# Chunked attention into a leaky-ReLU feed-forward: first-layer products of blocks 5 to 8, sums in PSUM, and a new step order

## The chip, the cores and the metric

The kernel runs on one core of a Trainium2 chip. The time of a run is the device time of that core in microseconds (us). A run can be taken with a hardware profile; the profile's span goes from the first to the last instruction of the program, so the time of a run is a little longer than a span.

Five engines matter here. TensorE (PE in the profile, PEld for its weight loads) multiplies and writes only to PSUM, a small memory of eight banks that each hold 512 float32 numbers in each of 128 partitions. VectorE (DVE), ScalarE (ACT) and GpSimd (POOL) do elementwise work on the main on-chip memory, SBUF; the first two also read and write PSUM. SyncE (SP) issues transfers. POOL also issues those transfers that convert float32 to float16.

## The reference

```python
# q, k, v: (8 batches, 8 heads, 576, 64); chunks of 64 rows attend to themselves
scores = scale * np.matmul(q_c, k_c.transpose(0, 1, 2, 4, 3))
scores = scores - np.max(scores, axis=-1, keepdims=True)
attn = np.exp(scores)
attn = attn / (np.sum(attn, axis=-1, keepdims=True) + 1e-09)
out = np.matmul(attn, v_c)
# then x = out as (4608 tokens, 512 features)
h = x @ w_in                      # 512 -> 2048
g = np.maximum(0.01 * h, h)
return (g @ w_out).astype(np.float32)   # 2048 -> 512
```

## The kernel before

The 4608 tokens are worked in two rhythms. Attention goes by groups u = 0 to 35 of 128 tokens (two chunks of all eight heads). The feed-forward part goes by blocks j: two of 128 tokens, then 17 of 256 (`BLOCKS`, line 46), so a block from 2 on takes two groups.

A group passes through these steps, each a function and a letter of the order: `g` loads q and k with a conversion to float16; `tq` and `tk` transpose them on TensorE, `q` and `k` copy the transposes out of PSUM (from group 14 on the DMA transposes instead, `tdq` and `tdk`, and `cq` copies q into a buffer padded with zeros); `s` is the score product; `m`, `b`, `x`, `z`, `n` are maximum, subtraction, exponential, sum with reciprocal, and normalisation; the softmax is transposed either on TensorE (`e`, with a copy `c`) or by the DMA (`d`); `v` is the product with v, and `a` copies it into `xT`, the ring of transposed tokens. The steps `e`, `c` are used for groups 0 to 5 and `d` from group 6 on. `y` and `w` write zeros into the padded buffers at the start, and `i` multiplies ones into an unused bank: i33 stands for 33 units of 128 columns, in matmuls of up to three units. All `i` steps stand ahead of the first step of the first layer.

The second layer of blocks 2 to 18 uses seven block products in place of eight (the Strassen form of Winograd): `sum` forms four sums of the hidden values (SG, line 203), `R` is one product of 8 matmuls over 256 columns (`product`, line 205), `comb` copies or adds the parts (`combine`, line 251). The first layer uses it from block 9 on (`W0`, line 50): `xs` forms four sums of tokens, `V` is one product for one half s of the hidden features (`wide`, line 389, 8 matmuls over 128 columns), 14 to a block. There, products 1, 6, 7 and 4 add up in one bank, and after each of the first three `lx` (line 442) copies the running sum to SBUF (`xkeep`); products 2, 5 and 3 go to other banks and `la` (line 449) adds the kept copies to them on VectorE; `lp` and the last `lx` apply the leaky ReLU. Blocks 0 to 8 compute the first layer plainly: `A` and `M` (`mm1`, line 311) and the leaky ReLU `H` and `G` (`act1`, line 328). For blocks 5 to 8 that is eight steps M of 8 matmuls over 256 columns.

Nothing schedules at run time. The string `ORDER` (line 735) lists the steps, the program issues them in that order, and each engine works through its own instructions in that order, waiting where an operand is not ready. The loads of the first nine groups and of the weights are issued from a list of their own ahead of it (`LOADS`, line 142). PSUM is cut up by hand: four banks for products are dealt out by the digits of `BANKS` (line 154), and the other four belong to q transposes, k transposes, scores, and the softmax with its product, which products share in some blocks.

Of the kernel before, what the change touches and what calls it, by code (L numbers as in the profile page):

```python
# [16 lines left out]
def kernel(  # L17
# [24 lines left out]
    VL = (4, 5, 6, 7)  # L42
    UX = 9
    G = 2 * CH

    BLOCKS = 2 * [128] + 17 * [256]
    EARLY = (2, 3, 4)
    LAST = len(BLOCKS) - 1
    HF, HM = NFC // 2, d_model // 2
    W0 = 9  # L50
    AMID = range(W0, 17)
    ONE = EARLY + tuple(range(16, len(BLOCKS)))
    ZMM = range(W0 - 2, 16)

# [3 lines left out]


# [5 lines left out]
    xT = sbp.tile([128, NT, RING], FP16, name="xT")  # L65
    qk: dict[int, tuple[bass.AP, bass.AP]] = {}

    made: set[tuple] = set()

    def need(*what):  # L70
        assert what in made, what

    def load_qk(u):

        both = []
        for name, src in (("q_in", q), ("k_in", k)):
# [18 lines left out]
    def load_v_heads(b, m, h0, h1):  # L95
        if b >= NVB:
            need("batch", b - NVB)
        nc.gpsimd.dma_start(  # L98
            out=VB[b % NVB][m * CH:(m + 1) * CH, h0:h1, :, m * CH:(m + 1) * CH].rearrange("p h c d -> p (h c) d"),
            in_=v[b, m * H // 2 + h0:m * H // 2 + h1].rearrange("h (c j) d -> j (h c) d", j=CH),  # L100
        )

    def load_v(b):
        for m in range(2):
            load_v_heads(b, m, 0, H // 2)

    def load_w_in(f0, f1):
        for m in range(2):
            nc.gpsimd.dma_start(
                out=w_inT[m * CH:(m + 1) * CH, :, f0:f1],  # L110
                in_=moe_w_in[m * d_model // 2:(m + 1) * d_model // 2, f0:f1].rearrange("(t d) f -> d t f", d=D),
            )

    def load_w_in_quarter(a):
        load_w_in(512 * a, 512 * a + 512)

    def load_w_out_quarter(a):
        load_w_out(4 * a, 4 * a + 4)
# [33 lines left out]


    BANKS = (
        "01230123012301230123023123103210310231023102320132132013213021302132103120312031023102310320323123131232121321"
        "31321323213212132131321323213210213021320130201321"
    )
    banks = iter(BANKS)

    def mm():  # L160
        return "m" + next(banks)

    TW: dict[int, bass.AP] = {}
    SG: dict[tuple[int, int], bass.AP] = {}
    bank: dict[tuple[int, str], bass.AP] = {}
    kept: dict[tuple[int, str], bass.AP] = {}
    opened: set[tuple[int, str]] = set()

    def weight_sum(n):
        b11, b12 = w_outT[:, :HF, :HM], w_outT[:, :HF, HM:]  # L170
        b21, b22 = w_outT[:, HF:, :HM], w_outT[:, HF:, HM:]
        x, y = {1: (b12, b11), 2: (b22, TW.get(1)), 3: (b22, b12), 4: (b21, TW.get(2))}[n]
        TW[n] = sbp.tile([128, HF, HM], FP16, name=f"TW{n}")
        nc.vector.tensor_tensor(out=TW[n], in0=x, in1=y, op=ALU.subtract)

    def rows(j):

        nh = BLOCKS[j] // 2
        halves_of = slice(0, nh), slice(nh, 2 * nh)
        return halves_of[::-1] if j in EARLY else halves_of  # L180

    def token_sums(j, n):
        if (j, n) in SG:
            return
        if j in EARLY:
            for a, p in {
                1: [(a, 1) for a in range(4)], 2: [(0, 2), (1, 2)], 3: [(0, 1), (1, 1), (0, 2), (1, 2)], 4: [(2, 2), (3, 2)],
            }[n]:
                need("act", j, a, p)
        if n in (2, 4):  # L190
            token_sums(j, n // 2)
        nh = BLOCKS[j] // 2
        one, two = rows(j)
        a11, a12 = gT[j][:, :HF, one], gT[j][:, HF:, one]
        a21, a22 = gT[j][:, :HF, two], gT[j][:, HF:, two]
        SG[j, n] = sbp.tile([128, HF, nh], FP16, name="SG", tag="gS", bufs=4, padded_shape=[128, HF, 128])
        x, y, op = {
            1: (a21, a22, ALU.add),
            2: (SG.get((j, 1)), a11, ALU.subtract),
            3: (a11, a21, ALU.subtract),  # L200
            4: (a12, SG.get((j, 2)), ALU.subtract),
        }[n]
        (nc.gpsimd if (j, n) in SG_POOL else nc.vector).tensor_tensor(out=SG[j, n], in0=x, in1=y, op=op)  # L203

    def product(j, n, i):
        one, two = rows(j)
        g, w = gT[j], w_outT
        where, left, right = {
            1: ("X", g[:, :HF, one], w[:, :HF, :HM]),
            2: ("W", g[:, HF:, one], w[:, HF:, :HM]),  # L210
            3: ("Z", SG.get((j, 4)), w[:, HF:, HM:]),
            4: ("X", g[:, HF:, two], TW.get(4)),
            5: ("Z", SG.get((j, 1)), TW.get(1)),
            6: ("X", SG.get((j, 2)), TW.get(2)),
            7: ("X", SG.get((j, 3)), TW.get(3)),
        }[n]
        if where != "X" and j in ONE:
            where = n
        if (j, where) not in bank:
            tag = None if j in EARLY else {"X": "qp", "Z": None if j in ZMM else "kp"}.get(where)  # L220
            bank[j, where] = psp.tile([128, 2, HM], FP32, name=f"pr{where}", tag=tag or mm(), bufs=1)
        to = bank[j, where]
        if j == LAST and n == 4:
            last_product(left, right)
            return
        for f in range(HF):
            nc.tensor.matmul(  # L227
                out=to[:, i, :],
                lhsT=left[:, f, i * 128:(i + 1) * 128],
                rhs=right[:, f, :],  # L230
                start=(j, where) not in opened,
# [119 lines left out]
    def w_in_sum(n):  # L351
        if len(WS) >= n:
            return
# [519 lines left out]
```

## Time and profile before

| What | Value |
|---|---|
| Median of three runs | 275.13 us (274.96 to 275.59) |
| Span of the profiled execution | 273.3 us |
| First layer begins | 17.44 us |
| Instructions | 9009 |
| HBM read, written | 36.70 MB, 9.44 MB |

The profile gives the span alone for its execution; the runs' times also hold what lies around it. An engine's busy time counts compute only. A matmul's end is modelled, and the next one starts before it, so the step from one start to the next, not a matmul's own length, is what a matmul costs.

### The profile page before, as it was taken

To read this page: it belongs to the slowest core of one execution; us is meant where nothing else is said; L and a number is where in the kernel's file an instruction comes from. 1 tells how busy PE (TensorE), PEld (TensorE's weight loads), DVE (VectorE), ACT (ScalarE), POOL (GpSimd) and SP (SyncE) were. 2 spreads that over 40 slices of the span, in tenths; PEclk is the share of its full clock that TensorE was granted. 3 is DMA by queue.
4 is the path that set the end of the run, shared out by engine and by line. 5 is a ranking of instruction groups with operands and counts; after the bars stand their busy time and mean duration, and the time that the engine had idled before them with its cause. 6 is when DMAs were issued, how large, how long until landed. Compare 5 with 4: busy or idle time off the path is not lost.

```text
span 273.3 us, 9009 instructions
## 1 busy us (share of the span) xinstructions
PE 265.9 (97%) x3705; PEld 242.4 (89%) x3705; DVE 219.9 (80%) x427; ACT 208.8 (76%) x410; POOL 165.3 (60%) x190
## 2 busy tenths in 40 slices
PE   7889999999999999999999999999999999999994
PEld 3579958999999899998989999999999998999994
DVE  7786869999997668798677987977899879488783
ACT  6667635665779688666999989899999998857560
POOL 8848546783175448649689799689895636012100
PEclk9999999999999999999999999999999999999999
DMA  9999999999999999999999999799999503131113
GB/s 147 155 188 191 206 178 156 176 117 130 210 138 169 171 140 119 195 219 168 164 189 153 203 160 124 139 134 180 95 147 158 134 2 101 22 98 40 41 41 115
DMA packets 159241, 38.34 MB, mean 140 GB/s; under 512 B 150240, under 2 KB 154720, under 8 KB 159200
## 3 DMA queue, kind: packets, MB, share of 16 engines
q0 software_dynamic: 111392, 18.10, 98.3%
q1 hardware_dynamic: 46768, 19.41, 38.7%
q8 instruction: 29, 0.48, 0.7%
q10 hardware_dynamic: 1040, 0.26, 0.4%
q14 instruction: 12, 0.10, 0.2%
HBM read 36.70 MB, written 9.44 MB: 169 GB/s over the span
## 4 chain that ended last, share of the span: by engine, by line
PE 86%; DVE 5%; ACT 3%; POOL 3%; issue 2%; POOLq 0%; DVEq 0%; ACTq 0%
PE hT L319 20%; PE prX L227 20%; PE xbank L416 11%; PE xpr L416 9%; PE prZ L227 6%; PE pr L227 6%; PE prW L227 3%; PE Sp L584 3%; PE xp L656 3%; PE oP L462 3%; ACT QZ L539 1%; ACT gT L435 1%; PE kp L512 1%; PE qp L512 1%; POOL SG L203 1%
## 5 line engine op out<-in xcount | busy, mean ns | idle before, releaser
L319 PE MATMUL hT<-xT,w_inT 128*128 128x128 f16 (+1 forms) x768 | 62.4, 237 | 0.0
L319 PEld LDWEIGHTS <-w_inT 128*128 128x128 f16 x768 | 53.6, 98 | 2.8
L227 PEld LDWEIGHTS <-SG 128*128 128x128 f16 x544 | 51.0, 98 | 5.4
L620 POOL TENSOR_TENSOR en<-ex,zi 128x512 f16<-128x512 f16 x26 | 28.2, 1085 | 40.1 <-DVE zi L614 19.8
L453 DVE TENSOR_TENSOR xkeep<-xpr,xkeep 128x512 f32<-128x512 f32 x60 | 39.6, 681 | 13.7 <-ACT xkeep L447 9.6
L333 ACT ACTIVATE gT<-hT 128x512 f16<-128x512 f32 x64 | 36.6, 595 | 9.0 <-PE hT L319 8.9
L227 PEld LDWEIGHTS <-gT 128*128 128x128 f16 x400 | 37.3, 98 | 4.3 <-ACT gT L435 0.4
L447 ACT ACTIVATE xkeep<-xbank 128x512 f32<-128x512 f32 x60 | 34.6, 593 | 7.4 <-PE xbank L416 7.0
L416 PEld LDWEIGHTS <-WS 128*128 128x128 f16 x640 | 38.0, 98 | 0.5
L91 POOL DMA_DIRECT2D q_in<-in_q_dram x39 | 33.4, 861 | 7.0 <-DMA w_outT<-in_moe_w_out_dram 3.0
L91 POOL DMA_DIRECT2D k_in<-in_k_dram x39 | 32.6, 838 | 7.8 <-DMA VB<-in_v_dram 3.3
L227 PE MATMUL prX<-TW,SG 128*128 128x256 f16 x272 | 35.3, 273 | 0.0
L435 ACT ACTIVATE gT<-xkeep 128x512 f16<-128x512 f32 x56 | 33.4, 631 | 2.1 <-DVE xkeep L453 1.8
L260 ACT ACTIVATE keep<-prX 128x256 f32<-128x256 f32 x51 | 19.6, 384 | 16.9 <-PE prX L227 16.5
L416 PEld LDWEIGHTS <-w_inT 128*128 128x128 f16 x480 | 29.0, 98 | 0.9 <-issue 0.4
L203 DVE TENSOR_TENSOR SG<-gT 128x1024 f16<-128x1024 f16 x34 | 25.2, 740 | 4.7 <-ACT gT L333 2.9
L610 DVE TENSOR_REDUCE z<-ex 128x8 f32<-128x512 f16 x36 | 24.4, 679 | 4.9 <-ACT ex L604 4.7
L593 DVE TENSOR_REDUCE mx<-Sp 128x8 f32<-128x512 f32 x36 | 24.4, 677 | 4.5 <-PE Sp L584 4.5
L573 ACT ACTIVATE QZ<-QT 64x512 f16<-64x512 f16 x44 | 27.3, 627 | 0.9 <-PE Sp L584 0.3
L677 ACT ACTIVATE xT<-xp 128x512 f16<-128x512 f32 x36 | 21.5, 596 | 6.0 <-PE xp L656 5.8
L387 POOL TENSOR_TENSOR xs<-xT 128x256 f16<-128x256 f16 x18 | 12.5, 701 | 20.7 <-ACT xT L677 20.7
L98 POOL DMA_DIRECT2D VB<-in_v_dram x24 | 23.4, 987 | 0.0
(92 smaller groups left out, 486.0 us busy)
## 6 DMA issues: line engine op xcount, KB each, us to landing
out_dram<-osb SPq DMA_DIRECT2D x35, 256.0 KB, 4.1
q_in<-in_q_dram POOLq DMA_DIRECT2D x31, 128.0 KB, 5.9
k_in<-in_k_dram POOLq DMA_DIRECT2D x31, 128.0 KB, 6.7
VB<-in_v_dram POOLq DMA_DIRECT2D x8, 288.0 KB, 9.1
VB<-in_v_dram POOLq DMA_DIRECT2D x16, 144.0 KB, 5.3
w_inT<-in_moe_w_in_dram POOLq DMA_DIRECT2D x8, 256.0 KB, 7.2
w_outT<-in_moe_w_out_dram POOLq DMA_DIRECT2D x4, 512.0 KB, 11.6
q_in<-in_q_dram POOLq DMA_DIRECT2D x8, 64.0 KB, 6.3
```

What stands on the lines that cost most here:

```text
L91: nc.gpsimd.dma_start(out=to, in_=rows)
L203: (nc.gpsimd if (j, n) in SG_POOL else nc.vector).tensor_tensor(out=SG[j, n], in0=x, in1=y, op=op)
L227: nc.tensor.matmul(out=to[:, i, :], lhsT=left[:, f, i * 128:(i + 1) * 128], rhs=right[:, f, :], start=(j, where) not in opened, stop=(f == ...
L319: nc.tensor.matmul(out=hT[:, i, :], lhsT=w_inT[:, t, fc * 128:(fc + 1) * 128], rhs=xT[:, t, r0:r0 + tb], start=(t == 0), stop=(t == NT - 1),)
L333: nc.scalar.activation(out=gT[j][:, nf * a:nf * a + nf, c0:c0 + tb], in_=HT.pop((j, a, p)), func=AFT.Prelu, bias=0.0, scale=1.0, alpha=0.01,)
L416: nc.tensor.matmul(out=to[:, i, :], lhsT=left[:, t, i * 128:(i + 1) * 128], rhs=right[:, t], start=(n in (1, 2, 5) and t == 0 and i == 0), ...
L435: nc.scalar.activation(out=gT[j][:, f0:f0 + 4, hi * 128:hi * 128 + 128], in_=of, func=AFT.Prelu, bias=0.0, scale=1.0, alpha=0.01)
L447: nc.scalar.activation(out=XK[j, s, n], in_=XB[j, s], func=AFT.Copy, bias=0.0, scale=1.0)
L453: nc.vector.tensor_tensor(out=to, in0=of, in1=to, op=ALU.add)
L573: nc.scalar.activation(out=to, in_=QT[u][part], func=AFT.Copy, bias=0.0, scale=1.0)
L593: nc.vector.tensor_reduce(out=MX[u], in_=SP[u], axis=AXL.X, op=ALU.max)
L620: (nc.gpsimd if u >= UP else nc.vector).tensor_tensor(out=E[u], in0=ex, in1=ZI.pop(u).unsqueeze(2).to_broadcast((128, 8, CH)), op=ALU.mult)
```

## The change

The program is rewritten so that every tile's place is read from one string. The eight PSUM banks form one pool, and the digits of `BANKS` name the bank of each PSUM tile and the slot of each rotating SBUF tile. A step that ends in `'` goes to its second engine: VectorE in place of ScalarE for copies and the leaky ReLU, POOL in place of VectorE for `n`, `xs` and `sum`, ScalarE in place of VectorE for the small add `z.1` and for the zeros `y`. `z` is split into three steps. Blocks 0 to 4 keep plain first layers, and blocks 5 to 18 use seven products. `e` and `c` serve groups 0 to 8, and `d` the others.

In the seven products, the first product is copied into a second PSUM bank (`ls`), onto which product 2 is then accumulated; product 5 is copied to SBUF (`lf`); `la` with 3 adds the running sum to it and writes that into the bank on which product 3 is then accumulated, and `la` with 7 adds the running sum once more in SBUF. The four results go through the leaky ReLU as they stand (`lp`).

```diff
-    W0 = 9
-    ONE = EARLY + tuple(range(16, len(BLOCKS)))
+    LATE = (2, 3, 4)
+    FIVE = (2, 3, 4, 16, 17, 18)
...
+    def copy(other, to, of):
+        if other:
+            nc.vector.tensor_copy(out=to, in_=of)
         else:
+            nc.scalar.activation(out=to, in_=of, func=AFT.Copy, bias=0.0, scale=1.0)
...
-        if n in (1, 6, 7, 4):
-            if n == 1:
-                tag = "kp" if s else "Sp"
-                if j in AMID:
-                    tag = "m0" if s else "kp"
-                XB[j, s] = psp.tile([128, 4, 128], FP32, name="xbank", tag=tag, bufs=1)
-            to = XB[j, s]
-        elif n == 3:
-            to = XM[j, s, n] = XM[j, s, 5]
-        else:
-            to = XM[j, s, n] = psp.tile([128, 4, 128], FP32, name="xpr", tag=mm(), bufs=1)
+        if n == 1:
+            XB[j, s] = ps([128, 4, 128], "xbank")
+        elif n == 5:
+            XZ[j, s] = ps([128, 4, 128], "xz")
+        to = {2: XW, 3: XZ, 5: XZ}.get(n, XB)[j, s]
...
-    def wide_x(j, s, n):
-        if n == 4:
-            leaky(j, s, 0, 1, XB.pop((j, s)))
-            return
-        XK[j, s, n] = sbp.tile([128, 4, 128], FP32, name="xkeep", tag="xkeep", bufs=6)
-        nc.scalar.activation(out=XK[j, s, n], in_=XB[j, s], func=AFT.Copy, bias=0.0, scale=1.0)
+    def wide_seed(j, s, other=0):
+        XW[j, s] = ps([128, 4, 128], "seed")
+        copy(other, XW[j, s], XB[j, s])
+
+    def wide_five(j, s, other=0):
+        X5[j, s] = sb([128, 4, 128], FP32, "x5", "xkeep", 6)
+        copy(other, X5[j, s], XZ[j, s])
...
-    def wide_m(j, s, n):
-        of = XM[j, s, n]
-        to = XK[j, s, {2: 1, 5: 7, 3: 6}[n]]
-        nc.vector.tensor_tensor(out=to, in0=of, in1=to, op=ALU.add)
+    def wide_add(j, s, n):
+        to = XZ[j, s] if n == 3 else X5[j, s]
+        nc.vector.tensor_tensor(out=to, in0=XB[j, s], in1=X5[j, s], op=ALU.add)
+
+    def wide_leaky(j, s, n, other=0):
+        second, hi = {2: (0, 0), 4: (0, 1), 3: (1, 0), 5: (1, 1)}[n]
+        of = {2: XW, 4: XB, 3: XZ, 5: X5}[n][j, s]
...
     ORDER = (
-        "i33 y4 y2 I y0 y6 y1 tq0 q0.0 q0.1 w3 tk0 i5 k0 i6 s0 tq1 i4 m0 b0 q1.1.1 i13 tk1 q1.0.1 x0 k1 tq2 i8 s1 tk2 "
-        "z0 m1 b1 k2.1 n0 i6 q2.0.1 q2.1.1 x1 i9 i7 i13 e0 c0.1 z1 s2 tk3 v0 tq3 m2 n1 b2 a0 e1 c1 i7 v1 A0.0 x2 a1 "
+        "y4' y2' g1 i2.1 i16.2 g2 i73.0 I If tq0 y3' y0' q0.0' i4.9 tk0 tq1 i4.7 k0' y1' q0.1 q1.1' tq2 q2.0' q1.0 s0 "
+        "q2.1 g3 tk1 k1 L0 tq3 q3.1 s1 tk2 tk3 i5.3 i12.4 m0 b0 x0 Q0 m1 z0.0 k2 Q1 z0.1' b1 x1 z0.2 s2 m2 z1.0 q3.0 "
+        "z1.1' k3 i47.5 b2 z1.2 x2 n0' e0 i3.6 n1 s3 i3.8 e1 c0 v0 m3 z2.0 z2.1 z2.2 c1 v1 b3 a0 M0.0.0 a1 M1.0.0 n2 x3 "
...
-        "comb18.6 R18.3.0 comb18.0 comb18.3 comb17.3 R18.7.0 comb18.7 R18.2.0 comb18.5 comb18.2 R18.4.0 comb18.4 "
+        "comb18.6 R18.7 st17.0 comb17.5 comb17.4' comb18.7' R18.4 comb18.5 st18.1.1 st17.1 R18.3 comb18.0 comb18.3 R18.2 "
+        "comb18.2 st18.0 "
```

The list `LOADS` is gone, and loads are steps of the order (`g`, `L`, `Q` for a quarter of w_in, `P` for a quarter of w_out). Counts over both orders: matmul steps R 119 and 119, V 140 and 196, plain steps over 256 columns 32 and 0, plain steps of 16 matmuls over 128 columns 32 and 32, softmax transposes on TensorE 6 and 9, fillers 111 and 169 units. The number after the point of a filler step is not used.

More of the change, by code (lines that the diff above doesn't have):

```diff
@@ L176, in rows @@
[L176 to L183, printed above, removed]
-            return
[L185 to L224, printed above, removed]
-            return
[L226 to L231, printed above, removed]
-                stop=(f == HF - 1),
-                skip_group_check=True,
-            )
-            opened.add((j, where))
@@ L735, with stage_a, hidden, part_of @@
-    ORDER = (
[84 rows of a table removed]
+    def stage_a(u, other=0):
+        at = u * G % RING
+        copy(other, xT[:, :, at:at + G], XP[u])
+        groups.add(u)
+    gT: dict[int, bass.AP] = {}
+    HT: dict[tuple[int, int, int], bass.AP] = {}
+    def hidden(j):
+        if j not in gT:
+            gT[j] = sb([128, NFC, BLOCKS[j]], FP16, "gT", "gT", 3, padded_shape=[128, NFC, NB])
+        return gT[j]
+    def part_of(j, p):
+        return (128, (p - 1) * 128) if p else (BLOCKS[j], 0)
+    def mm1(j, a, p=0):
+        tb, c0 = part_of(j, p)
+        rows_ready(START[j] + c0, START[j] + c0 + tb)
+        r0 = (START[j] + c0) % RING
+        nf = 512 // tb
+        hT = ps([128, nf, tb], "hT")
+        for i in range(nf):
+            fc = nf * a + i
+            for t in range(NT):
+                nc.tensor.matmul(
+                    out=hT[:, i, :],
+                    lhsT=w_inT[:, t, fc * 128:(fc + 1) * 128],
+                    rhs=xT[:, t, r0:r0 + tb],
+                    start=(i == 0 and t == 0),
+                    stop=(t == NT - 1),
+                    skip_group_check=True,
+                )
+        HT[j, a, p] = hT
@@ new lines, in wide_seed @@
+    def wide_seed(j, s, other=0):
[10 more added lines that the diff above has]
+        of = {2: XW, 4: XB, 3: XZ, 5: X5}[n][j, s]
+        f0 = 8 * s + 4 * second
+        leaky(other, hidden(j)[:, f0:f0 + 4, hi * 128:hi * 128 + 128], of)
@@ new lines, in product @@
+    def product(j, n):
+        one, two = halves_of(j)
+        g, w = gT[j], w_outT
+        where, left, right = {
+            1: ("X", g[:, :HF, one], w[:, :HF, :HM]),
+            2: ("W", g[:, HF:, one], w[:, HF:, :HM]),
+            3: ("Z", SG.get((j, 4)), w[:, HF:, HM:]),
+            4: ("X", g[:, HF:, two], TW.get(4)),
+            5: ("Z", SG.get((j, 1)), TW.get(1)),
+            6: ("X", SG.get((j, 2)), TW.get(2)),
+            7: ("X", SG.get((j, 3)), TW.get(3)),
+        }[n]
+        if where == "Z" and j in FIVE:
+            where = f"Z{n}"
+        if n in (1, 2, 5) or where == "Z3":
+            bank[j, where] = ps([128, HM], f"pr{where[0]}")
+        to = bank[j, where]
+        if j == LAST and n == 4:
+            last_product(left, right)
+            return
+        for f in range(HF):
+            nc.tensor.matmul(
+                out=to,
+                lhsT=left[:, f, :],
+                rhs=right[:, f, :],
+                start=(f == 0 and (n in (1, 2, 5) or where == "Z3")),
+                stop=(f == HF - 1),
+                skip_group_check=True,
+            )
@@ new lines, in mm2, with plain_out, store @@
+    def mm2(j, ti, part):
+        if part == 0:
+            oP[j, ti] = ps([128, d_model], "oP")
+        for fc in range(part * 4, part * 4 + 4):
+            nc.tensor.matmul(
+                out=oP[j, ti],
+                lhsT=gT[j][:, fc, ti * 128:(ti + 1) * 128],
+                rhs=w_outT[:, fc, :],
+                start=(fc == 0),
+                stop=(fc == NFC - 1),
+            )
+    def plain_out(j, ti, other=0):
+        copy(other, output(j, ti), oP[j, ti])
+    def store(j, t, c=2):
+        r0 = START[j] + (t * 128 if j in PLAIN else halves_of(j)[t].start)
+        cut = slice(0, d_model) if c == 2 else slice(c * HM, c * HM + HM)
+        nc.sync.dma_start(out=out[r0:r0 + 128, cut], in_=ob[j, t][:, cut])
```

657 lines of the change are left out of this document (252 added, 405 removed), and 166 rows, old and new, of the table ORDER.

## The prediction

> **What bounds the kernel now.** I read the page first (busy shares, then the chain), then the windows, then the chain piece by piece.
>
> ```profile
> span 273.3 us, 9009 instructions
> PE 265.9 (97%) x3705; PEld 242.4 (89%) x3705; DVE 219.9 (80%) x427; ACT 208.8 (76%) x410; POOL 165.3 (60%) x190
> PE 86%; DVE 5%; ACT 3%; POOL 3%; issue 2%; POOLq 0%; DVEq 0%; ACTq 0%
> ```
>
> TensorE is busy 97% of the span, and 86% of the chain that ends last is its own work. Where it is idle stands in the windows of 10 us:
>
> ```profile
> 0.00:10.00 10.00, 7.65 (x83) 4.44 (x85) 6.74 (x14) 5.93 (x8) 8.88 (x17) 1.00 1.53 148
> 10.00:20.00 10.00, 8.75 (x166) 6.72 (x159) 8.91 (x19) 7.03 (x12) 5.39 (x9) 1.00 1.70 177
> ...
> 140.00:150.00 10.00, 9.82 (x150) 9.21 (x148) 7.24 (x13) 9.48 (x20) 9.92 (x12) 1.00 1.83 157
> ...
> 200.00:210.00 10.00, 9.98 (x156) 9.44 (x155) 9.55 (x16) 9.26 (x21) 8.10 (x9) 1.00 1.87 136
> ...
> 220.00:230.00 10.00, 9.91 (x154) 9.21 (x151) 8.95 (x19) 8.58 (x18) 4.15 (x5) 1.00 0.23 69
> ...
> 260.00:273.30 13.30, 9.76 (x113) 8.79 (x111) 8.42 (x17) 4.84 (x11) 0.00 (x0) 1.00 0.23 80
> sum 273.30, PE 265.88 PEld 242.36 DVE 219.92 ACT 208.84 POOL 165.27; mean PE 9.85 PEld 8.98 DVE 8.15 ACT 7.73 POOL 6.12
> ```
>
> The first figure after the length is TensorE's busy time. Of 273.30 - 265.88 = 7.42 us idle, 3.60 lie before 20 us, 3.54 after 260 (behind the last matmul), and 0.29 in all the 240 us between. So the time is the start, plus the sum of TensorE's work, plus the tail. A step saved on TensorE is worth its whole length, unless something else then ends last.
>
> **The change, part by part.** *Products.* Blocks 5 to 8 compute the first layer with 8 steps M of 8 matmuls over 256 tokens each; now with 14 steps V of 8 matmuls over 128. The chain in order of time gives both, running without a gap:
>
> ```profile
> 91.03 0.87 PE hT L319 x8
> ...
> 145.25 0.89 PE xbank L416 x16
> ```
>
> Plain: 8 x 0.87 = 6.96 us a block. Seven products: 14 x 0.89/2 = 6.23. Four blocks save 4 x 0.73 = **-2.9**. Blocks 9 to 18 keep their matmuls (10 x 14 steps before and after, and 119 steps R both times); only where their sums are made differs.
>
> The Trainium skill (TensorE: Matmul & The Clock Gate, section "Back-to-back issue gap") speaks against this: it gives about 81 ns for each matmul of 128 columns in a real stream with weight loads. By that figure the 112 matmuls of a converted block would take an estimated 9.1 us and lose 2.1 to the plain form. The row above says 0.89 us for 16, 56 ns each, weight loads included, so the measurement decides for the saving.
>
> *Softmax transposes.* e6, e7, e8 come back from the DMA queue to TensorE: 3 x 4 transposes of 128 columns at 56 ns = **+0.7**. Their three copies (0.4 us on VectorE, 0.6 on ScalarE) lie beside matmuls; three DMA transposes fewer on SP were off the chain.
>
> *Start.* The order holds filler matmuls (step i, in units of 128 columns). Before: 33 units ahead of the first transposes tq0, then 78 up to the first layer. After: i2, i16, i73 = 91 units ahead of tq0, then again 78. The timeline of the start:
>
> ```profile
> 1.33 3.50 PE L686 MATMUL idle<-warm 128*128 128x384 f16 x11 [1.33 <-DVE zeros L137]
> ...
> 4.71 0.63 PE L512 MATMUL qp<-ident,q_f 128*128 128x128 f32 x4
> ...
> 11.59 2.07 PE L686 MATMUL idle<-warm 128*128 128x384 f16 x13
> ...
> 17.44 1.95 PE L319 MATMUL hT<-xT,w_inT 128*128 128x128 f16 x32
> ```
>
> The first 33 units run slowly (3.50 us), later ones take 2.07/35 = 0.059 us (13 matmuls of i6, i9, i7 and i13). So the 58 extra units put tq0 off by 58 x 0.059 = 3.4 us, to 8.1. That is the upper end if each later wait stays as it was. The lower end: TensorE idles 3.60 - 1.33 = 2.3 us between its first matmul and 20 us; were all of that swallowed, 1.1 is left, and 0.2 less because s3 is now done ahead of the first layer: +0.9. Walking the new order with durations from the timeline (tq0 8.1, score s0 at 10.2, e0 behind i47 at 16.6, e1 17.5, v1 18.5, M0.0.0 at about 19.0 against 17.44) I get 1.5 later, less the 0.2 of s3: **+1.3**. The zeroing that moves from VectorE to ScalarE lies under the filler. n0 moves to POOL and stands there ahead of g4, g5 and the third quarter of w_in, which in the walk is needed within a microsecond of landing: if that cover goes, up to +1.
>
> *Sums.* For each half s of a wide block, three ScalarE copies to SBUF and three VectorE adds become one copy into a PSUM bank as the seed of product 2 (ls), one copy of product 5 (lf), and two adds (la3, la7). Product 3 now waits for la3, product 2 for ls, and products 6, 7, 4 queue behind ls, la3, la7 on TensorE; behind a late la3 stand all later matmuls. The rows that price these (in the groups by line):
>
> ```profile
> L453 DVE TENSOR_TENSOR xkeep<-xpr,xkeep 128x512 f32<-128x512 f32 x60 | 39.6, 681 | 13.7 <-ACT xkeep L447 9.6 <-PE xpr L416 3.9
> ...
> L447 ACT ACTIVATE xkeep<-xbank 128x512 f32<-128x512 f32 x60 | 34.6, 593 | 7.4 <-PE xbank L416 7.0 <-DMA out_dram<-osb 0.2
> ...
> L620 POOL TENSOR_TENSOR en<-ex,zi 128x512 f16<-128x512 f16 x26 | 28.2, 1085 | 40.1 <-DVE zi L614 19.8 <-ACT xkeep L447 9.8 <-ACT gT L435 3.0
> ...
> L573 ACT ACTIVATE QZ<-QT 64x512 f16<-64x512 f16 x44 | 27.3, 627 | 0.9 <-PE Sp L584 0.3
> L203 DVE TENSOR_TENSOR SG<-gT 128x1024 f16<-128x1024 f16 x34 | 25.2, 740 | 4.7 <-ACT gT L333 2.9 <-ACT gT L435 1.8
> ...
> L203 POOL TENSOR_TENSOR SG<-gT,SG 128x1024 f16<-128x1024 f16 x8 | 17.4, 2173 | 9.3 <-DVE SG L203 4.0 <-ACT keep L260 2.7 <-ACT xkeep L447 2.6
> ...
> L281 DVE TENSOR_TENSOR osb<-prZ,keep 128x256 f32<-128x256 f32 x22 | 9.3, 421 | 4.6 <-PE prZ L227 3.1 <-ACT keep L260 1.2
> ...
> L387 DVE TENSOR_TENSOR xs<-xT 128x256 f16<-128x256 f16 x2 | 0.6, 282 | 0.0
> ```
>
> Counted over both orders, VectorE gains 21 second-layer copies (at 0.42, nearest row L281, +8.8), 12 seed and product-5 copies and 9 xT copies (at 0.68, row L453, +14.3), 10 QZ copies (0.2 to 0.63; 0.42, +4.2), 19 token sums xs (0.28, +5.4) and 7 normalisations (0.7, +4.8); it gives up 10 SG sums (-7.4), 4 adds (-2.7), the zeroing (-4.6) and 21 small adds (-3.8); key and query copies leave about +1.5. That is about +20: 240 of some 272 us, 88% instead of 80%. ScalarE falls by about 20, POOL gains 10 SG sums of 2.17 and loses 7 en and 3 xs, +12. All three stay under TensorE, so in the likeliest case the idle time in the middle stays near 0.3: **0**. Its bounds: -0.3 (all gone), and the rival below.
>
> *Tail.* The last matmuls before are a product cut in two halves of 128 columns:
>
> ```profile
> 268.70 1.06 PE L244 MATMUL prL<-TW,gT 128*128 128x128 f16 x16
> ...
> 269.80 0.29 DVE L248 TENSOR_TENSOR osb<-prL,keep 128x128 f32<-128x128 f32 x1 [0.15 <-PE prL L244]
> 269.87 0.89 SPq L249 DMA_DIRECT2D out_dram<-osb  x2
> ```
> ```profile
> out_dram<-osb SPq DMA_DIRECT2D x35, 256.0 KB, 4.1
> ...
> out_dram<-osb SPq DMA_DIRECT2D x2, 64.0 KB, 1.7
> ```
>
> Now product 2 comes last: its add is 0.13 longer (0.42), but SP has no earlier issue to finish (-0.2), and it stores 256 KB at once. Between 1.7 and 4.1 us to land; the queue is nearly empty there, so near 2.1: **+0.3** (bounds 0 to +2.3).
>
> **Sum.** -2.9 + 0.7 + 1.3 + 0 + 0.3 = -0.6 on the profiled 273.3. The median of the runs is 275.13, 1.8 above that span, for launch and end; the same difference gives 275.13 - 0.6 = 274.5.
>
> **Rivals.** *VectorE becomes the bound (slower).* The windows:
>
> ```profile
> 40.00:75.00 35.00, 35.00 (x527) 32.67 (x526) 33.01 (x69) 21.84 (x44) 20.36 (x24) 1.00 2.44 158
> 75.00:180.00 105.00, 104.82 (x1365) 97.03 (x1364) 84.94 (x165) 88.96 (x177) 76.25 (x84) 1.00 1.61 161
> ```
>
> VectorE is at 94% from 40 to 75 already. The new order lists more of it there: its steps between the second layer of block 1 and the first product of block 4 add up to 30.5 us beside 30.7 of matmuls, counting 0.61 for a full-width add issued behind another. Where adds wait on each other the whole 0.68 counts, 11% more: 3.4 us over in this stretch. It decides from the point where VectorE's lag is more than the eight PSUM banks hold, since the next product then waits for its add. Against it: the same engine at 94% delayed nothing before. Also, an SG sum can be held up by POOL:
>
> ```profile
> 204.40 1.98 DVE L203 TENSOR_TENSOR SG<-gT 128x1024 f16<-128x1024 f16 x1
> ...
> 204.76 1.06 POOL L620 TENSOR_TENSOR en<-ex,zi 128x512 f16<-128x512 f16 x1
> ```
>
> 1.98 instead of 0.68, and POOL gets 12 us more such work. SBUF: State Buffer in the Trainium skill ("shared port pair") calls this an exclusive lock for a whole instruction; by it each meeting with the 2.17 us POOL sums would cost up to that, and this row agrees. Price 3 us: 277.5.
>
> *The filler is paid in full (slower).* Each wait after tq0 is a latency chain, so all 3.4 us stay: 274.5 + 2.1 = 276.6. For it: en waits for VectorE before e0 at the start. Against it: 2.3 us of idle lie there to be used.
>
> *Less is paid (faster).* The start at its lower end, the 0.3 in the middle gone: 274.5 - 0.4 - 0.3 = 273.8. With nothing paid anywhere, 275.13 - 2.2 = 272.9; rows rounded to 0.01 on 56 steps leave 0.4 more.
>
> *The products do not pay (slower).* The groups give a weight load as long as
>
> ```profile
> L416 PEld LDWEIGHTS <-WS 128*128 128x128 f16 x640 | 38.0, 98 | 0.5
> ```
>
> If a matmul of 128 columns had to wait for its whole load, a converted block would take 112 x 0.098 = 11.0 us, 4.0 over the plain form: 275.13 + 16.1 + 2.3 = 293.5. The row at 145.25 speaks against it: loads are hidden at 56 ns a matmul. By the skill's 81 ns from the same section the estimate would be 285.8 instead.
>
> **How the numbers follow.** What this kernel's measurement can tell from no change is about 0.2%, 0.55 us. Forecast 0.44 (own range 273.9 to 275.2: 0.24 faster, 0.19 same, 0.01 slower); less is paid 0.20 (0.19 faster, 0.01 same); VectorE 0.22 (0.21 slower, 0.01 same); filler in full 0.12 (0.11 slower, 0.01 same); products 0.02 slower. Faster 0.43, same 0.22, slower 0.35. The range goes from 272.5 to 278.5 (VectorE's price of 3 and the uncertain 1 of the third quarter).
>
> **What would show it.** Right: M0.0.0 near 19.0 us, xbank and xz steps at 0.89 for 16 from block 5 on, middle idle under 0.5 us, last matmul 1.7 earlier minus the start's delay. Wrong: TensorE idle between 40 and 180 with la or SG on VectorE as releaser; tq0 well before 8 us; a last store that lands 4 us after its issue.

## The result, and the profile after

The changed kernel takes **284.54 us** (median of 4 runs, 283.61 to 287.02) beside 275.36 for the kernel before (274.96 to 275.85): a ratio of 1.0343, 95% interval 1.0293 to 1.0392. It is 9 us slower; 0.6 less was forecast. The profiled run took 283.91, its span 282.0. The runs of the changed kernel spread over 1.2%, those of the kernel before over 0.3%. All times and ratios below are of fast runs alone, which leaves out a run more than 1.5% above the shortest of its kernel.

The page after: span, busy times, then TensorE and its granted clock in 40 slices, then the head of the chain.

```profile
span 282.0 us, 9449 instructions
PE 268.7 (95%) x3928; PEld 246.8 (88%) x3928; DVE 227.9 (81%) x468; ACT 193.2 (69%) x383; POOL 175.3 (62%) x190
PE   8799999999599999998999999979999999999994
PEclk9979999999889999999999999999999999999999
DMA  9999999999999999999999999999995225002033
PE 81%; DMA 8%; DVE 4%; POOL 3%; issue 2%; ACT 1%; SPq 0%; POOLq 0%; DVEq 0%; ACTq 0%
```

TensorE's row has two dips (5 and 7), the clock's row two (7, and 88), and a DMA with 8% stands in a chain that had none of it before. TensorE's waits, with total, number and longest:

```profile
PE xp L335 <- DMA et<-en: 5.1, 2, 3.4
PE Sp L277 <- ACT KT L200: 1.8, 1, 1.8
PE idle L194 <- DVE tiny L166: 1.3, 1, 1.3
PE xbank L442 <- DVE xz L461: 0.9, 1, 0.9
```

The first is new: two products xp wait for softmax transposes by DMA. The chain from 66 to 80 us, in order of time (start, length, what), and TensorE's row there in the timeline:

```profile
67.52 1.05 POOL en L309
68.57 0.02 issue
68.59 7.72 DMA et<-en
76.31 0.14 issue
76.44 0.59 PE xp L335 x8
77.03 1.71 PE hT L370 x16
```
```profile
76.44 0.59 PE L335 MATMUL xp<-et,VB 128*128 128x64 f16 x8 [3.44 <-DMA et<-en]
```

This is v9. Its transposes d9 were issued at 68.59 and landed at 76.31. Only 1.1 us of matmuls stand between the two in the order (the 16 of M4.2.2 and group 8's transposes). That alone does not make them late: in the kernel before only 0.87 us (R4.7.0) stands between the same two steps. What counts is how much work TensorE still has ahead of the product when the transposes are issued. The same two operations before:

```profile
71.39 1.21 SPq L643 DMA_TRANSPOSE et<-en  x1
...
79.22 0.40 PE L656 MATMUL xp<-et,VB 128*128 128x64 f16 x8
```

There TensorE worked for all of the 7.83 us between them, and the transposes landed after 5.97, with a slack of 1.87. Now it works for 4.41 of the 7.85, and they land after 7.72.

The second product, v24, is late for another reason. Its normalised softmax, on GpSimd, and the chain behind its transposes:

```profile
164.40 1.04 POOL L309 TENSOR_TENSOR en<-ex,z 128x512 f16<-128x512 f16 x1
```
```profile
179.38 7.22 DMA et<-en
186.60 0.05 issue
186.65 0.41 PE xp L335 x8
```

The softmax was ready at 165.44, and d24 was issued 13.9 us later, since it stands that far behind n24 in the order; only 1.3 us of matmuls are listed between it and v24. A place nearer to n24 was not tried.

After the wait at v9 even the matmuls are slow: 16 of hT, which take 0.89 at full clock, take 1.71. The windows (length, TensorE, weight loads, VectorE, ScalarE, GpSimd, clock, DMA, GB/s) show why, at the start of the kernel and here:

```profile
12.00:14.00 2.00, 1.14 (x42) 0.98 (x42) 1.27 (x2) 1.93 (x4) 0.00 (x0) 1.00 1.76 171
14.00:16.00 2.00, 1.94 (x16) 1.13 (x15) 1.49 (x4) 1.59 (x4) 0.26 (x1) 0.67 1.23 202
16.00:18.00 2.00, 2.00 (x8) 0.99 (x7) 1.97 (x5) 1.60 (x5) 2.00 (x3) 0.50 1.18 195
...
74.00:76.00 2.00, 0.00 (x0) 0.00 (x0) 0.67 (x2) 0.93 (x2) 2.00 (x2) 1.00 2.53 153
76.00:78.00 2.00, 1.56 (x20) 1.59 (x21) 0.00 (x0) 0.00 (x0) 2.00 (x2) 0.53 2.53 154
78.00:80.00 2.00, 2.00 (x19) 1.69 (x18) 0.00 (x0) 0.60 (x1) 1.04 (x1) 0.62 1.71 117
```

Behind each of these two idle stretches the clock is near half for 3 to 4 us. Where the time came from, with each matmul of the trace counted at the undisturbed duration of its form (56 ns for 128 columns of f16, 109 for 256) and the rest of its distance to the next as lost:

| us | before | after | difference |
|---|---|---|---|
| matmuls that compute | 255.87 | 253.58 | -2.3 |
| filler, and lost up to 30 us (the start) | 11.39 | 15.09 | +3.7 |
| lost from 30 us on | 0.96 | 8.11 | +7.1 |
| last matmul's end to the end | 3.5 | 3.6 | +0.1 |

The sum, +8.6, is the difference of the spans (282.0 - 273.3 = 8.7) to rounding. Of the 8.1 us lost from 30 us on, the wait at v9 has 3.6 and the half clock behind it 1.4, a wait at 130 has 1.1, and v24 at 185 has 1.8.

### The profile page after: what moved, and what is told of

It is laid out like the page before. It is cut to its first block, busy times and chain, and to the rows that moved or that the text cites. A ratio compares the mean times of both kernels' runs of the same rounds, so it can differ in the third digit from the quotient of the medians.

```text
span 282.0 us, 9449 instructions
## 1 busy us (share of the span) xinstructions
PE 268.7 (95%) x3928; PEld 246.8 (88%) x3928; DVE 227.9 (81%) x468; ACT 193.2 (69%) x383; POOL 175.3 (62%) x190
## 4 chain that ended last, share of the span: by engine, by line
PE 81%; DMA 8%; DVE 4%; POOL 3%; issue 2%; ACT 1%; SPq 0%; POOLq 0%; DVEq 0%; ACTq 0%
PE prX L525 18%; PE xbank L442 16%; PE prZ L525 10%; PE xz L442 8%; DMA et<-en 8%; PE hT L370 7%; PE prW L525 5%; PE idle L194 4%; PE seed L442 4%; PE xp L335 3%; PE oP L571 2%; PE Sp L277 2%; POOL VB L122 1%; DVE z L303 1%; POOL SG L502 1%
## 5 line engine op out<-in xcount | busy, mean ns | idle before, releaser
L442 PEld LDWEIGHTS <-WS 128*128 128x128 f16 x896 | 54.8, 98 | 2.1 <-DVE xz L461 1.2
L442 PEld LDWEIGHTS <-w_inT 128*128 128x128 f16 x672 | 40.9, 98 | 0.5
L442 PE MATMUL xbank<-xs,WS 128*128 128x128 f16 x448 | 33.0, 219 | 0.9 <-DVE xz L461 0.9
L502 POOL TENSOR_TENSOR SG<-gT,SG 128x1024 f16<-128x1024 f16 x9 | 19.3, 2145 | 22.8 <-PE prZ L525 11.9
L370 PE MATMUL hT<-xT,w_inT 128*128 128x128 f16 x512 | 32.9, 222 | 0.1
L370 PEld LDWEIGHTS <-w_inT 128*128 128x128 f16 x512 | 30.2, 99 | 0.2 <-issue 0.2
L309 POOL TENSOR_TENSOR en<-ex,z 128x512 f16<-128x512 f16 x19 | 20.5, 1079 | 14.9 <-DVE z L305 13.1
L384 ACT ACTIVATE gT<-xz 128x512 f16<-128x512 f32 x28 | 16.6, 596 | 9.4 <-PE xz L442 7.6
L461 DVE TENSOR_TENSOR xz<-xbank,x 128x512 f32<-128x512 f32 x28 | 19.0, 693 | 4.0 <-PE xbank L442 3.1
L384 ACT ACTIVATE gT<-hT 128x512 f16<-128x512 f32 x32 | 17.8, 594 | 6.4 <-PE hT L370 6.0
L384 ACT ACTIVATE gT<-seed 128x512 f16<-128x512 f32 x28 | 16.6, 596 | 7.8 <-PE seed L442 6.9
```

What stands on the lines that cost most here:

```text
L309: (nc.gpsimd if other else nc.vector).tensor_tensor(out=EN[u], in0=EX[u], in1=Z[u, 2].unsqueeze(2).to_broadcast((128, 8, CH)), op=ALU.mult)
L370: nc.tensor.matmul(out=hT[:, i, :], lhsT=w_inT[:, t, fc * 128:(fc + 1) * 128], rhs=xT[:, t, r0:r0 + tb], start=(i == 0 and t == 0), stop=( ...
L384: nc.scalar.activation(out=to, in_=of, func=AFT.Prelu, bias=0.0, scale=1.0, alpha=0.01)
L442: nc.tensor.matmul(out=to[:, i, :], lhsT=left[:, t, i * 128:(i + 1) * 128], rhs=right[:, t], start=(n in (1, 5) and t == 0 and i == 0), st ...
L461: nc.vector.tensor_tensor(out=to, in0=XB[j, s], in1=X5[j, s], op=ALU.add)
L502: (nc.gpsimd if other else nc.vector).tensor_tensor(out=SG[j, n], in0=x, in1=y, op=op)
```

## The experiments

The theory at first: waits for late DMA transposes and the fall of the clock behind them cost the middle; the filler costs the start. Its rival: VectorE is behind. Each run is told with its ratio to the kernel before.

### One cause at a time

**e1**: group 9 goes through TensorE.

```
- ... s11 d9 z10.1 q13.0 sum3.3 n8 q13.1 G4.3.1 ...
+ ... s11 z10.1 q13.0 sum3.3 n8 q13.1 e9 c9' G4.3.1 ...
```

> Group 9 goes back to TensorE transposes (e9, then c9 on VectorE); all else as in the changed kernel. Theory A (the 3.6 us wait ahead of v9 is the DMA transpose of group 9, and the slow matmuls behind it are the clock that fell in the wait): the wait of 3.4 us on the DMA and the 1.4 us of half-rate matmuls behind it both go, 4 to 5 us less in the span, granted clock 1.00 from 70 to 80 us. Theory B (VectorE is behind in this stretch, and v9 is only the place where it shows): TensorE waits for VectorE there or a few us later instead, and less than 2 us is won.

281.88, ratio 1.0235 (1.0186 to 1.0283). The wait at v9 is gone and with it the half-rate stretch, as theory A said, and no new wait for VectorE there or behind it is longer than 0.4; but only some 2.7 us are won of the 4 to 5: group 11's transposes, with slack of 1.1 in the changed kernel, are late now. The chain of e1 there:

```profile
84.97 8.17 DMA et<-en
93.14 0.05 issue
93.19 0.41 PE xp L335 x8
```

**e2**: loads and transposes of groups 17 and 18 go behind d9's critical time.

```
- ... z10.0 g17 M4.0.2 tdq16 ...  G4.0.2 tdq17 G3.2.2 v9 tdk17 ...  G4.2.2 g18 st1.0 tdq18 ...
+ ... n10' g17 g18 ...  d10 tdq17 tdk17 tdq18 ...
```

> The loads of groups 17 and 18, four of the six issued between 68.5 and 74 us, are moved behind the normalisation of group 10, and their own transposes behind d10. If the loads in flight make the transpose of group 9 slow (7.7 us from issue to landing), it lands in 5 to 6 us, the wait before v9 falls from 3.6 to about 1.5 us and the clock stays up: 2.5 to 4 us less. If the transpose is late for its late issue alone (68.6 us), it takes 7 to 8 us as before and the wait stays at 3 us or more.

284.26 (two runs), ratio 1.0320 (1.0265 to 1.0375). d9 landed in 5.46 us instead of 7.72 and v9 waited 1.2 instead of 3.4, so loads in flight do slow it; but the longest wait was then v11's, 2.8, and nothing clear of the noise was won.

**e3**: group 9's softmax sooner, on VectorE.

```
- ... z9.2 G4.1.1 G4.2.1 n9' ... s11 d9 ...
+ ... z9.2 n9 d9 G4.0.1 ...
```

> The last small step of the softmax sum of group 9 (z9.2) and its normalisation, moved from POOL to VectorE, stand right behind z9.1 in the order, and d9 behind them. If the place in VectorE's queue made d9 late, d9 issues near 66 us instead of 68.6 and 2.5 us of the wait go, with the half-rate stretch: 3 to 5 us less. If VectorE is full (theory B), the steps pushed back cost as much again within 10 us.

288.45 (two runs), ratio 1.0472 (1.0416 to 1.0527): slower still. The profile is of a longer run (292.30), whose start had slipped by 2 us, where nothing was changed (first layer at 23.76). Against its first layer d9 came 1.0 us sooner than in the changed kernel, and v9 waited 1.6 instead of 3.4; the loss came later, with waits of 3.0 for a sum at 132 and of 4.3 at v24. So the place in VectorE's queue is a part of d9's lateness, and what made the runs slower is not settled.

**e4**: 58 filler units fewer.

```
- ... g2 i73.0 I If tq0 ...
+ ... g2 i15.0 I If tq0 ...
```

> The filler i73 is cut to i15, so that 33 units stand ahead of the first transposes as in the kernel before. If the filler is what moved the start, the first transposes begin at 5.0 to 5.3 us instead of 7.8 and the first layer at 18.5 to 19.3 instead of 21.7, 2.5 to 3 us less in the span. If the loads or the softmax chain end last in the start, the first layer begins at 21 us or later all the same.

279.72, ratio 1.0155 (1.0114 to 1.0196): half of the loss is back. The first transposes stand at 5.04 as before the change, yet the first layer only at 21.22 (after: 21.74), since the clock fell from 10 us on and the fixed 47 units ran at half rate:

```profile
12.00:14.00 2.00, 1.94 (x36) 1.23 (x31) 1.92 (x4) 1.58 (x4) 0.00 (x0) 0.50 1.59 179
14.00:16.00 2.00, 2.00 (x15) 1.18 (x13) 0.60 (x2) 1.22 (x2) 1.88 (x3) 0.50 1.22 199
16.00:18.00 2.00, 2.00 (x10) 0.98 (x8) 1.97 (x5) 1.25 (x3) 2.00 (x4) 0.62 1.30 200
```

The rest was won in the middle: the transfers ahead of d9 landed sooner (the second load of V ahead of it in 5.5 us instead of 7.9), d9 itself landed in 4.3, and v9 did not wait. Against the first layer they were issued no sooner; why fewer were in flight is not shown.

**e6**: 20 of those 47 units go ahead of score s1, into the idle stretch.

```
- ... q3.1 s1 tk2 ...  k3 i47.5 b2 ...
+ ... q3.1 i20.5 s1 tk2 ...  k3 i27.6 b2 ...
```

> Of the 47 filler units ahead of the transposes of group 0, 20 are put ahead of score s1, where TensorE is idle for 1.8 us in the changed kernel; the sum of filler units stays. Theory (the idle stretch makes the granted clock fall, and the filler behind it, at half rate, ends last): the clock stays at 1.00 from 10 to 20 us, the remaining 27 units take 1.6 us, the transposes of group 0 begin near 17 instead of 19.3 and the first layer near 19.5 to 20.3 instead of 21.7; the time falls by 1.5 to 2. Rival (the first layer is set by the chain of queries, scores and softmax, not by filler): the first layer stays at 21 or later and the time falls by under 0.5.

284.82, ratio 1.0337 (1.0291 to 1.0384): no gain in the time. The first layer came at 21.16, as the rival said, but not for the rival's reason alone. The clock stayed at 1.00 and the filler was fast, so that the stretch from tq0 to the first layer took 12.24 us instead of 13.97, as the theory said. But tq0 itself came at 8.92 instead of 7.77, with the same steps ahead of it: TensorE got through 8 matmuls between 4 and 6 us here and through 13 in the changed kernel's profile. In e7 and e9, where the filler stands as in the changed kernel and the clock stayed at 1.00 all the same, the same stretch takes 12.40 and 12.39, so the move itself is worth under 0.2.

**e7**: one small add goes to ScalarE.

```
- ... V8.0.6 V8.1.1 z18.1 R7.2 ...
+ ... V8.0.6 V8.1.1 z18.1' R7.2 ...
```

> The small add of step z18.1 (128x8) goes from VectorE to ScalarE. In the changed kernel it takes 2.06 us instead of 0.16 at 128.7, beside GpSimd's issue of two loads, and TensorE then waits 0.9 for a sum of block 8 that stands behind it on VectorE. If that wait is the small add's, the time falls by 1.0 to 1.3 and no wait above 0.3 is left between 125 and 133; if the wait is VectorE's backlog, another operation is late there and the time stays within 0.4.

Not settled: of four runs three took 285.67 to 286.76 and one 281.24, too far apart for a ratio. In the profile, of a run of 285.67, VectorE's next operation stood idle in its place, 3.2 us, though the matmul it is put down to was long done; that looks like its output buffer, which a store frees, but this is argued, not shown:

```profile
132.46 0.42 DVE L563 TENSOR_TENSOR ob<-prW,keep 128x256 f32<-128x256 f32 x1 [3.21 <-PE xz L442]
```

### Five groups on TensorE

**e5**: groups 9, 11, 20, 23 and 24 as in e1. **e8**: the same with e6 and e7. **e9**: the same five with the copies of the last four on ScalarE and better banks. **e10**: e9 with e6, e7 and the 15 units of e4.

```
e5  d11 -> e11 c11'   d20 -> e20 c20' (behind R8.7)   d23 -> e23 c23' (behind x27)    d24 -> e24 c24' (behind lp12.0.2)
e9  d11 -> e11 c11    d20 -> e20 c20  (behind R8.7)   d23 -> e23 c23  (behind R9.3)   d24 -> e24 c24  (behind R10.3)
```

> Softmax groups 9, 11, 20, 23 and 24 are transposed by TensorE (5 times 4 transposes, 0.22 us a group, with their copies on ScalarE) and no longer by the DMA. Theory (the DMA transposes land after TensorE has come to their product, because the new order leaves 1 to 4 us of matmuls between the two): the waits ahead of products v9 and v24 (3.4 and 1.7 us) and the half-rate stretch behind v9 (1.4) go, the other DMA transposes, with slack of 1.4 us and more, stay hidden, 1.1 us of transposes come; the time falls by 5 to 6 us to about 279, and no matmul after 40 us waits for a DMA by more than 0.5. Rival (the softmax itself comes late because VectorE is behind): TensorE then waits ahead of the transposes for en, and the time stays within 2 us of the changed kernel's.

> The three edits above together. If the three causes are separate and the whole of the loss in the middle: 284.5 - 5.5 - 1.7 - 1.1 = about 276, with no wait above 0.5 us behind 40 us and a granted clock of 1.00 in every stretch. If they hide one another (each wait removed lets TensorE reach the next DMA transpose earlier, which then is late): 279 or more, with new waits at other groups' products.

> Groups 9, 11, 20, 23 and 24 are transposed by TensorE again, but the copies of 11, 20, 23 and 24 now stand on ScalarE (in the run before of five groups all five stood on VectorE, in order ahead of a seed copy and the sums; VectorE stood idle 3.6 us for group 20's transposes), group 23's transposes use a bank that is read earlier, and group 24's stand one product later. Theory (late DMA transposes, and the copies' queue in the run before): the waits of 2.6 us at 150, 1.3 at 174 and 0.9 at 186 go, none of the products v9, v11, v20, v23, v24 waits over 0.3; what is left is the start as in the changed kernel and the 1 us at 128; time about 279 to 280. Rival (the order has no room for either form: any transposes at these places stop an engine): new waits of together 3 us or more in the same places, 283 or more.

> The same five groups on TensorE, 20 of the 47 filler units ahead of score s1, the small add z18.1 on ScalarE, and 15 instead of 73 filler units ahead of the first transposes (33 in all, as in the kernel before). Theory: the waits go as above; the start is as short as the chain of its softmax allows, with the first layer near 17.5 to 19; 255 of work + 9.4 of filler + 3 to 5 of waits + tail 3.6: a span of 271 to 274, a time of 273 to 276. If the gain at the start is given back at the next transfers (the load of V for group 9 landed 0.7 us late in the run of three edits, the transposes of group 10 just in time): 277 to 279.

e5: 286.83, ratio 1.0399 (1.0352 to 1.0445); e8: 283.64, 1.0293 (1.0256 to 1.0330). A prime on c means VectorE, not ScalarE as the expectation has it: c20' stood there in order ahead of a seed copy. The waits of e5, in a profile of its longest run (288.05), whose first layer came only at 24.40:

```profile
PE seed L442 <- DVE seed L198: 2.4, 1, 2.4
...
PE tpe L316 <- ACT ex L294: 1.2, 1, 1.2
```

The second is a bank whose last reader stood right ahead. No wait for a DMA transpose is left, but these took its place. With both mended, e9: 281.63, ratio 1.0209 (1.0155 to 1.0264), the clock at 1.00 in all slices, 4.1 us lost behind 30 us instead of 8.1. That is 2.9 won, where theory said 4.5 to 5.5, and 1.1 us of what the profile shows is the start, where nothing was changed: the first layer came at 20.67 instead of 21.74, since the clock did not fall.

e10: 279.29, ratio 1.0122 (1.0057 to 1.0188). Its first layer starts at 18.06; the only difference to e6 and e8 in what stands ahead of it is the 58 units. These have it at 21.16 and 20.38, so with the clock held the units cost 2.3 to 3.1 us, most of their 3.4. The longest waits of e10 behind the start:

```profile
PE prZ L525 <- ACT gT L384: 1.2, 1, 1.2
PE tpe L316 <- ACT gT L384: 0.8, 1, 0.8
PE xp L335 <- DMA VB<-in_v_dram: 0.6, 1, 0.6
PE xbank L442 <- DVE ob L563: 0.6, 1, 0.6
```

No product waits for a softmax transpose any more, and the filler is that of the kernel before. Yet by the count of the table some 5 us are lost from 30 us on, where the kernel before loses 0.96. So late transposes are what costs the changed kernel most in the middle, but with them gone its order still loses time, to ScalarE, VectorE and a load.

### The theory on the kernel before

**e11**: in the kernel before, two transposes go later, nothing else.

```
- ... la10.1.3 d23 lp10.0.1.0 ...   comb10.4 d25 lp11.0.1.0 ...
+ ... R10.2.0 d23 V11.0.6 ...   R11.2.0 d25 v24 ...
```

> The kernel before, with nothing changed but the place of two DMA transposes: those of softmax groups 23 and 25 stand 3 to 4 us of matmuls later in the order, so that about 4.4 us of matmuls are left ahead of their products (before: some 8; landing took 5.3 and 4.4 us there, with slack of 1.9). Theory: v23 and v25 wait for them, 0.5 to 2 us each, and the granted clock falls behind a long wait; the time rises by 1.5 to 3.5 us. Rival (what slows the changed kernel is not the place of its transposes but something else in its new order): the two waits stay under 0.3 and the time within 0.6 of the kernel before.

277.35 (10 runs), ratio 1.0057 (1.0031 to 1.0082): 1.9 us slower, inside the theory's 1.5 to 3.5. The profile is of the shortest of the ten runs (275.88); it has one wait, at v23, shorter than the 0.5 to 2 forecast for each of the two:

```profile
167.25 0.41 PE L656 MATMUL xp<-et,VB 128*128 128x64 f16 x8 [0.43 <-DMA et<-en]
```

### Products later, and what then comes late

**e12**: in the changed kernel the five products move, the transposes stay. **e13**: e12 with the start of e10 and one store sooner.

```
e12  v9 behind R3.5, v11 behind V6.0.1, v20 behind R8.4, v23 behind s28, v24 behind V12.1.7
e13  + i15, i20.5 ahead of s1, st5.1 behind st5.0
```

> The changed kernel with nothing moved but five products xp on TensorE: v9 (behind R3.5, some 4 us of matmuls later), v11 (1.3 later), v20 (2.2), v23 (0.7) and v24 (0.9); every transpose stays on the DMA, where it was issued. Theory (the transposes are late only because their products stand too near): the wait of 3.4 us at v9 and the half-rate stretch behind it go entirely, that at v24 falls from 1.7 to under 1, v11, v20 and v23 wait for nothing; the time falls by 4.5 to 6 us to 279 to 280, more than with group 9 on TensorE (2.1 less) since no other group gets nearer its bound. Rival (the DMA queue is what limits, and any gain upstream comes back at the next transposes): 282 or more.

> The five products later as above, 20 of 47 filler units ahead of score s1, 15 instead of 73 units ahead of the first transposes, and the store of block 5's second half ahead on SyncE, right behind that of its first half (the combination of block 7 that waits 3.2 us on VectorE at 126 in two runs may wait for its output buffer, which that store frees). Theory: first layer at 18 as in the run of all edits; no wait above 1 us behind 40 us; a span of 253.6 + 9.7 of filler + 2.5 to 4.5 of waits + 3.6 = 269.5 to 271.5, a time of 271.5 to 274, below the kernel before. If the gain at the start comes back at transfers: 275 to 278.

e12: 285.99, ratio 1.0340 (1.0298 to 1.0383). The rival holds: v9 waited for nothing, and TensorE waited 3.9 at 84 us, behind another transfer. The timeline of e12:

```profile
86.61 0.63 ACT L200 ACTIVATE QZ<-QT 64x512 f16<-64x512 f16 x1 [4.95 <-DMA QT<-q_in]
...
87.62 0.36 ACT L200 ACTIVATE keep<-prX 128x256 f32<-128x256 f32 x1
...
88.04 0.37 PE L525 MATMUL prX<-TW,SG 128*128 128x256 f16 x1 [3.86 <-ACT keep L200]
```

ScalarE stands 4.95 us for group 15's transposed queries, and TensorE behind a copy that is queued after them. Those transposes stood on SyncE behind group 17's, which wait for a load issued at 68.6 and landed at 77. e13: 277.79 (six runs), ratio 1.0091 (1.0058 to 1.0124): level with e10, without its extra transposes.

**e14**: e12 with group 15 ahead. **e15**: e13 with group 15 ahead and the load of group 28 later.

```
e14  g15 behind L2 (was behind g17);  tdk15 tdq15 ahead of tdq17 (were behind tdk17)
e15  + g28 behind xs10.2'
```

> The five products later, as in e12, and the loads of group 15 ahead of that of group 17 on GpSimd (behind the load of V), with the DMA transposes of group 15's keys and queries ahead of those of group 17 on SyncE; there they stood behind the transposes of group 17, which wait for a load issued at 68.6 and landed at 77, so that ScalarE waited 5 us for group 15's queries and TensorE 3.9 behind it. Theory (the in-order queue of SyncE and the late loads ahead of it): both waits go, the half-rate stretch at 84 too; the time falls by 3.5 to 5 against e12, to 282 to 283. Rival (the DMA's rate is the bound: what is brought ahead of one transfer delays another): the wait comes back within 20 us at V's load, group 9's, 10's or 11's transposes; 285 or more.

> All that removed a wait without adding work: the products later, group 15 ahead, the filler (15 ahead of the first transposes, 20 of 47 ahead of score s1), the store of block 5's second half sooner, and the load of group 28 behind the token sums of block 10 on GpSimd (TensorE waited 1.8 us for them at 147 in e13). Theory: the two waits of e13 (2.2 at 82, 1.8 at 147) go; a span of 273, a time of 274.5 to 276, level with the kernel before. If waits come back elsewhere: 277.5 to 279.5.

e14: 283.05, ratio 1.0260 (1.0218 to 1.0302), 2.9 better than e12, a little less than the theory's 3.5 to 5. e15: 279.18 (five runs), ratio 1.0107 (1.0073 to 1.0140), no better than e13. In both profiles, which are of longer runs (286.68 and 280.25), the wait of e12 is gone and group 11's transposes land too late (9.4 and 9.1 us after their issue, slack 0.04); in e15 a product also waits 1.8 us for a load of V at 52.

### Fewer bytes

**e16** and **e17**: in the changed kernel and in the kernel before, half of each load of V from the third batch on is left out.

```
     def load_v_heads(b, m, h0, h1):
+        h1 = (h0 + h1) // 2 if b >= 2 else h1
```

> The changed kernel, with every load of V from the third batch on cut to half of its heads (the other half of the output is computed from older values); no instruction is added, moved or left out, only bytes. Theory (the DMA's rate: transfers are served in the order of their issue, and a softmax transpose lands when the loads issued before it are through): group 9's transposes, issued behind two loads of V that landed 6.1 and 7.9 us after their issue, land in 5 to 6 us instead of 7.7; the waits at products v9, v24 and at 130 shrink to together under 2.5 us (6.3 before), and the time falls by 3 to 6 us, to 278.5 to 281.5. Rival (the place of the transposes and SyncE's queue alone, whatever the load): landing and time stay within 1 us of the changed kernel's.

> The same cut of the loads of V in the kernel before. Theory: its transfers land 1.5 us and more ahead of their use, so sooner landing is worth nothing: 275.0 to 275.6, within 0.3 of the kernel before. Rival (the DMA's rate bounds the kernel before too): faster by 1 us or more.

e16: 281.91, ratio 1.0272 (1.0229 to 1.0315), 2.6 better; e17: 275.04, ratio 0.9986 (0.9965 to 1.0006), nothing. The DMA issues of d9 and its neighbours (median us from issue to landing), after and in e16:

```profile
q_in<-in_q_dram POOLq DMA_DIRECT2D x1, 128.0 KB, 7.4
k_in<-in_k_dram POOLq DMA_DIRECT2D x1, 128.0 KB, 7.3
et<-en SPq DMA_TRANSPOSE x1, 7.7
```
```profile
q_in<-in_q_dram POOLq DMA_DIRECT2D x1, 128.0 KB, 5.8
k_in<-in_k_dram POOLq DMA_DIRECT2D x1, 128.0 KB, 5.8
et<-en SPq DMA_TRANSPOSE x1, 6.0
```

Loads on GpSimd's queue and a transpose on SyncE's, issued together, land together, and sooner when less stands ahead of them. Not every transpose gained: group 20's took 7.6 us instead of 6.5. Group 9's wait fell to 1.8 us, and the clock did not fall behind it. The time fell by a little less than the 3 expected, and the intervals of e16 and of the changed kernel overlap; that the same bytes are worth nothing in the kernel before is the clearer half.

## Why the prediction was wrong, point by point

- **What bounds the kernel: half right.** TensorE's work, the start and the tail were named as the sum, and 0.29 us of idle in 240 was taken as a property of the kernel. It was one of the old order: there every softmax transpose from group 9 on landed 1.48 us or more ahead of its product. The page's DMA row, at 9 nearly up to the end of the loads in both kernels, was not read.
- **Products, -2.9, and transposes on TensorE, +0.7: right.** Together -2.2; measured -2.3. The chain in the converted blocks shows matmuls at the forecast price, 16 in 0.89, and the rival that products do not pay falls:

```profile
98.23 0.87 PE prZ L525 x8
99.10 0.89 PE xz L442 x16
```

- **"Three DMA transposes fewer on SP were off the chain", and the 0 in the middle: the step that failed.** True of the three, but the term of 0 was reasoned from the busy shares of VectorE, ScalarE and GpSimd alone. Whether the 27 DMA transposes that stay still land ahead of their products was not asked. For v9 TensorE's work behind the issue shrank from 7.83 to 4.41 us and the landing took 7.72; d24 stands 13.9 us behind a softmax that is ready. The term measured +7.1: 5.0 at v9 with the slow clock behind it, 1.8 at v24, 1.1 behind a VectorE operation at 130. The mends e1, e9 and e16 won 2.6 to 2.9 us of time, and e11 lost 1.9 in the other direction. That late transposes cost this time is shown; that they are the whole of it is not, since e10 has none and still loses 5.
- **Start, +1.3: mis-sized, +3.7 measured.** tq0 was forecast at 8.1 and came at 7.77. The first layer was forecast 10.9 us behind it, at 19.0, and came 13.97 behind it, at 21.74; in the kernel before that stretch took 12.73 (4.71 to 17.44). Two parts of the walk failed. The idle time swallowed next to none of the filler: in e9, with the same steps and the clock at 1.00, the stretch still takes 12.39. And the clock, which the walk held at full, fell to 0.50 behind the wait of 1.80, which makes the other 1.6. "The filler is paid in full", 276.6 with a chance of 0.12, was right in the first part of this.
- **VectorE becomes the bound: not borne out.** It was forecast at 240 us and 88%; the page has 227.9 and 81%. Of the 20 us that the count gave it more, 8.0 came. ScalarE (-15.6, forecast -20) and GpSimd (+10.0, forecast +12) were near. VectorE is not free of blame all the same: GpSimd's normalisation of group 9, right ahead of d9, waited 1.24 us for it. The one wait of TensorE behind a sum, 0.9, came with an operation that took 2.06 instead of 0.16; whether moving that operation (e7) wins anything is not settled.
- **Tail, +0.3: +0.1.** The last stores landed in 2.2 us, as estimated.

What stays open: no order tried brings the changed kernel under the one before; the best (e10, e13) stay 1% above. In e1, e2, e12 and e14 a wait that was taken away let TensorE reach another transfer that was late; in e10 other engines took its place. A wholly new order with the transfers' landing times in it was not tried, nor was d24 issued sooner, and e11's profile shows only 0.4 of its 1.9. The start is not the same from run to run either: with the same steps ahead of it, the first layer came between 20.57 (e7) and 24.40 us (e5), so a single run says little about 1 us.

## What to carry to other kernels

When an order is rearranged, look at each transfer's slack, not only at the engines: take from the trace the work that the busiest engine does between a transfer's issue and its first use, and set it against the landing time under load (here 7 to 8 us where it mattered, not the 2.4 of an empty queue). The work listed between the two steps in the order does not tell it, for the issuing engine may be far ahead of TensorE, as it was at d9 in the kernel before, or come to a transfer long after its data is ready, as at d24. A kernel with no idle time may have little slack to give, and a step that is faster brings every later transfer nearer. A wait of 3 us on TensorE can cost more than itself: behind the one of 3.44 at v9 the half clock took another 1.4.

## What the runs showed of the hardware

- **Landing depends on what is ahead, whatever queue issued it.** In the changed kernel softmax transposes land in 2.4 us at the soonest near the end, where few loads run, and in 3.0 to 8.4 between 60 and 190 us, behind loads that GpSimd issued. The Trainium skill (DMA: Bandwidth & Descriptors, section "Issuing engines are not separate DMA queues") says that DMAs of all engines run on the same 16 DMA engines and interleave; the three rows above, with 7.4, 7.3 and 7.7, agree.
- **The clock falls after shorter idle stretches than expected, and not always.** Behind 3.44 us of idle it was 0.53 and 0.62; behind 1.80 us at the start it fell to 0.50 in the changed kernel, and in e9, with the same wait of 1.8 and the same start, it stayed at full. A wait of 2.4 us for the same operation was followed by 0.50 in e5 and by 1.00 in e8, and waits of 2.2 and 2.7 in e6 by 1.00. The Trainium skill (TensorE: Matmul & The Clock Gate, "What's actually happening") gives an idle window of about 3.4 us that runs free of the kernel; the fall behind 3.44 fits, those behind 1.80 and 2.4 happen with less idle time than that, and the difference between two runs behind the same wait fits a window that runs free.
